# Gated mix of linear and softmax attention on one core: score groups of three and five, maxima units regrouped, one weight split on GpSimd, one PSUM pool fewer

## The chip, the cores and the metric

The kernel runs on one core of a Trainium2 chip. The engines of the core are PE (matmul, with its weight loads shown as PEld), DVE (vector), ACT (scalar), POOL (GpSimd) and SP, which here issues the DMA transfers. The metric is the device time of one execution in microseconds; the median of several runs counts.

## The reference

The input is x, 2048 tokens of 448 values. Two attentions with 16 heads of 28 run on it, and a gate mixes them, all in float32:

```
g   = sigmoid(x . gate_w)
A:  q, k, v = split(x @ A_wqkv);  pq, pk = q @ w_phi, k @ w_phi    (per head)
    phi = [softmax(p), softmax(-p)];  o = phi_q (phi_k^T v) / (phi_q sum(phi_k) + 1e-6);  a = o @ A_wo
B:  q, k, v = split(x @ B_wqkv);  o = softmax(q k^T * 28^-0.5) v;                       b = o @ B_wo
out = g * a + (1 - g) * b
```

Softmax is taken with its row maximum subtracted. In A that is cheap, as a row has 28 values; in B a row has 2048 scores, and the kernel finds the maxima in a pass of its own.

## The kernel before

Products of two float32 numbers are done in up to three matmul passes: every operand is split into a high part and the low rest (`XH`, `XL`; a weight has both parts side by side). `split_weight` (L141) writes the high part by a copy on ACT (L143) and the low part by a subtraction on DVE (L144); both engines can be given as arguments.

The order of the instructions on PE, DVE, ACT and POOL is that in which the program writes them (`manual_schedule`, L51); only the order of the transfers on SP is found by the planner. What stands ahead in a queue therefore holds what stands behind it.

**The front, 0 to some 336 us.**

- `proj_qk` (L577) makes queries and keys of B, 28 tiles of 11 passes each. ACT copies the high part of a tile (L589), DVE subtracts the low part (L590), and both go to DRAM (`qkd`).
- The loop over `i` (L727) has t = i and q = i − 16. For t below 16 it makes keys of A and their features (`features1`, `features2`, L438 to L462, on ACT, DVE and POOL), values of A (`value_a`), and adds to the key-value sums (`kv_add`). For q from 0 to 15 it makes queries and their features. From q = 3 it turns the features (`turn`, L515), multiplies them with the sums (`numer`), divides (`normalize1` to `normalize4`, whose last step writes `oTa` on POOL, L429), and multiplies with the output weight (`out_a`, tiles `poa`). From q = 18 it also makes the values of B (`value_b`, tiles `pvb`). Late in this loop, POOL's share is the feature subtraction (L447, L449), the feature product (L461) and `oTa`.
- At q = 2, the turn, the pools of the first half close and those of the second open. The PSUM pool is closed and opened there too, with four `s` banks in place of three and a `pv` bank.
- Forty-four **maxima units** (`mx_unit`, L259) lie between these pieces. A unit is four small matmuls into two double banks: `pmb` holds the scores against one half of a pair of key blocks, `pmd` those against the difference of the two. ACT takes the Relu of `pmd` (L288, `rl`), and two DVE instructions (L290) add `pmb` and keep the row maxima. The next unit's `pmb` waits for the Relu of the unit before it, its `pmd` for that unit's last reduce. Keys of a unit are prepared by two POOL subtractions (L221). `pace` and `tick` (L719) place one unit inside the matmul passes of a key and value pass; others stand at the head of steps, behind the feature work, or behind `out_a`.

**The main part, from some 336 us.** A step s (0 to 255) is one block of 128 keys against 512 queries for four heads. `scores` (L879) issues four matmuls into four PSUM banks (L885) and four exps on ACT (L903), whose results are kept in `p` tiles. `values` (L1010) of the step before adds eight small-column matmul pieces (L1017) into the `pv` bank. One `mx_visit` (L305) per step finds maxima for later heads: four matmuls `pm` (L322) into four banks, one `rl` on ACT from the first (L326), and DVE reduces (L333, L330, L336). The seven banks that scores and visits share stand in the list `free`; `mx_banks` takes four from its head, and `scores` puts used banks back in an order that sets which reader each later matmul waits for. Below s = 191 each step has four scores, values, visit. From 191, when `TWO` is reached, two steps' scores go together, with one visit, until the visits end; output projections (`project`, L1022) stand between the last steps.

Of the kernel before, what the change touches and what calls it, by code (L numbers as in the profile page):

```python
# [14 lines left out]
PSUM = bass.MemoryType.PSUM  # L15
DRAM = bass.MemoryType.DRAM

P = 128
S = 2048
D = 448  # L20
# [4 lines left out]
NT = S // P  # L25
# [15 lines left out]
def gated_mix_kernel(ctx, tc, xT, wqkB, wvB, wvA, wkAT, wqAT, phi, woA, woB,  # L41
# [17 lines left out]

    psn = [3, 2]  # L60

    def ps_s(nm):
        return ps.tile([P, 512], F32, tag="s", name=nm, bufs=psn[0])

    def ps_pv(nm):
# [546 lines left out]
    def split_part(w, key, n, i, low=nc.vector):  # L612
        split_weight(w, raws[key][i], slice(2 * i, 2 * i + 2), slice(0, n), low)

    def splits(n):

# [47 lines left out]
    for n in range(4, NP):  # L664
        take_acts()
        if n in (4, 5):
            x_loads(n - 2)
        if n == 8:
            nc.sync.dma_start(phi_s, phi)
            load_fold(wkAT, "k")  # L670
        if n == 10:
            part_loads("wB1", wqkB[:, :, 512:896], 384, "wB1")
        splits(n + 1)
        if n == 14:
            part_loads("wvA", wvA, 450, "wvA")
            nc.sync.dma_start(sel_s, sel)
            nc.sync.dma_start(mask_s, mask)
            for v in vap:
                nc.gpsimd.memset(v[:, :, 28:32], 0.0)
                nc.gpsimd.memset(v[:, :, 28:29], 1.0)  # L680
            feats = [bd.tile([P, H, 64], F32, name=f"feat{i}") for i in range(4)]
            for f in feats:
                nc.gpsimd.memset(f[:, :, 56:], 0.0)
        if 16 <= n < 20:
            mx_unit()
        proj_qk(n, ev)
        if n in (16, 18):
            split_part(wvA_s, "wvA", 450, (n - 16) // 2)
            take_lows()
        if 12 <= n < 16:  # L690
            fold(wkA_s, "k", n - 12)
        if n == 10:
            pair_query(0, 0)
            pair_load(0, 0)
        if n == 15:
            pair_load(0, 1)
            pair_query(0, 1)
        if n in (14, 19):
            take_subs()
# [27 lines left out]
    for i in range(2 * NT + 11):  # L727
        t, q = i, i - NT
        y = q - 1
        tb = y // 2  # L730
        take_acts()
        if t < NT and t % 2 == 0:
            mx_unit()
            passes = (55 if t < NT - 4 else 44) + (4 if t >= 4 else 0)
            pace["n"], pace["at"] = 4 if t >= 4 else 0, [passes // 2]
        if q in (0, 1):
            take_exps()

        if t % 2 == 0 and 0 <= t - 4 < NT:
            kv_add(t - 4)  # L740
            kv_add(t - 3)
        if q == 2:
            bk_s.close()
            ta_s = ExitStack()
            ta = ta_s.enter_context(tc.tile_pool(name="ta", bufs=1, reuse_waits="tile"))
            stg = ta_s.enter_context(tc.tile_pool(name="stg", bufs=2, reuse_waits="tile"))
            KV = ta.tile([P, 512], F32, name="KV")
            kvT = kv_copy()
            ps_s_.close()
            ps = ps_s_.enter_context(tc.tile_pool(name="psq", bufs=1, space=PSUM, reuse_waits="tile"))  # L750
            psn[0] = 4
            woA_s = weights(3, "woA_s")
            wvB_s = weights(2, "wvB_s")
            take_exps()
        if t < NT:
            pk = ps_s(f"pk{t}")
            tok_major(pk, t, wkA_s, D, tick)
            fk[t] = features1(pk, f"k{t}", nc.gpsimd)
            take_exps(1)
        if 0 <= q < NT:  # L760
            pq = ps_s(f"pq{q}")
            tok_major(pq, q, wqA_s, D)
        if q == 0:
            fk[NT - 1] = features2(fk[NT - 1], f"k{NT - 1}")
        if q in (1, 2):
            fq[q - 1] = features2(fq[q - 1], f"q{q - 1}")
        if 0 <= q < NT:
            fq[q] = features1(pq, f"q{q}", nc.vector if 0 < q < 9 else nc.gpsimd)
        if 0 <= t - 1 < NT - 1:
            fk[t - 1] = features2(fk[t - 1], f"k{t - 1}")  # L770
        if q in (0, 1) or q >= 8:
            mx_unit()
        if y >= 9 and y % 2 and tb - 4 < 8:
            oTs[tb - 4] = normalize4(ta, num.pop(tb - 4), f"a{tb - 4}", 2)
# [24 lines left out]
        if q == 2:  # L799
            raws["woA"] = [load_woA(b) for b in (0, 2)]  # L800
        if q == 11:
            part_loads("wvB", wvB, D, "wvB")
        if q in (4, 6):
            split_part(woA_s, "woA", D, (q - 4) // 2)
        if q in (14, 17):
            split_part(wvB_s, "wvB", D, (q - 14) // 3)
        if q == 1:
            gates()
        if y < 9 or y % 2:
            if y >= 2 and y - 2 < NT:  # L810
                turn(y - 2)
        if 0 <= y - 10 < NT:
            out_a(y - 10)
            out_a2(y - 10)
        if y >= 9 and y % 2 == 0 and y - 2 < NT:
            turn(y - 2)
        if NT + 3 <= q < NT + 10:
            mx_unit()
        if q == NT + 2:
            bd_s.close()  # L820
            vb = [value_tile(0)]
        if 0 <= q - NT - 2 < 8:
# [56 lines left out]
    def scores(s, i):  # L879
# [8 lines left out]
        if s == 0:  # L888
            p = at.tile([P, 2, 512], F32, tag="pp", name=f"p{s}_{i}", bufs=2)
            st = ps_mx(f"st{s}_{i}", i)  # L890
            for jl in range(2):
                score(2 * i + jl, st[:, jl, :])
            nc.scalar.activation(p, st, AF.Exp, scale=SCALE)
            pts.setdefault(s, []).extend([p[:, 0, :], p[:, 1, :]])
            return
        sts = []
        for j in (2 * i, 2 * i + 1):
            used.append(free.pop(0))
            sts.append(bank(used[-1], f"st{s}_{j}"))
            score(j, sts[-1])  # L900
        for j, st in enumerate(sts, 2 * i):
            p = p_slot(f"p{s}_{j}")
            nc.scalar.activation(p, st, AF.Exp, scale=SCALE)  # L903
            pts.setdefault(s, []).append(p)
        if i == 1:
            a, m = used[:], held[:]
            if s < TWO:
                free.extend([a[0], m[0], a[1], m[1], a[2], a[3], m[2]] if m else a)
            elif s % 2:
                free.extend([m[0], a[0], m[1], a[1]] if m else a)  # L910
                rest.extend([m[2], a[2], a[3]] if m else [])
            else:
                free.extend(rest + a)
                rest.clear()
            used.clear()
            held.clear()

    qst = [stack("qst0", False)]
    kst = [stack(f"kst{i}", True) for i in range(5)]
# [27 lines left out]

    free, used, held = list(range(7)), [], []  # L950
    spare, rest = [], []

    def bank(i, nm):
        return ps2.tile([P, 512], F32, tag=f"g{i}", name=nm, bufs=1)

    def mx_banks(f, first):
        b = [free.pop(0) for _ in range(4)]
        free.append(b[0])
        held.extend(b[1:])
        order = [first] + sorted({0, 1, 2, 3} - {first}, key=lambda j: j == first - 1)  # L960
        return [bank(b[order.index(j)], f"pm{f}_{j}") for j in range(4)]

# [59 lines left out]
    def project(qb, oT, tl):  # L1022
# [1 line left out]
        t = qb * 4 + tl  # L1024
        acc = acc_of[qb][:, tl, :]
        b = free.pop(0)
        free.append(held.pop(0) if held else b)
        if free[-1] != b:
            held.insert(0, b)
# [109 lines left out]
    for s in range(NS + 16):  # L1139
        take_acts()  # L1140
        if s < NS:
# [105 lines left out]
```

## Time and profile before

| | us |
|---|---|
| median of 3 runs | 1017.42 |
| lowest and highest run | 1017.32, 1019.32 |
| the profiled execution | 1015.89 |
| its span, first to last instruction | 1014.1 |
| granted PE clock | 1.000 |

Busy time in the span: PE 1002.8, ACT 815.7, DVE 679.7, PE's weight loads 561.9, POOL 236.0. A busy PE is not PE at its peak: the end of a matmul is modelled, so a small delay of the next one hides inside it. Delays of that size are therefore read from the starts of instructions, and larger ones from the waits. The timeline joins instructions of one kind that follow one another into one row, with their number at its end; the brackets tell how long the engine sat idle before it and what ended that.

### The profile page before, as it was taken

Reading aid. Unit: us, or ns where it says so; the run is one execution under the profiler, and the core shown is the slowest. Engines: PE = TensorE matmul, PEld = TensorE weight load, DVE = VectorE, ACT = ScalarE, POOL = GpSimd, SP = SyncE. Lnnn points to the kernel's source line nnn. Section 1 sums busy time; section 2 is a strip of 40 time slices with the busy share of each in tenths; the row PEclk is TensorE's granted clock in tenths of the full one; section 3 lists DMA queues with packets and bytes.
Section 4 is the critical chain, followed back from the end, with each engine's and each line's share of the span. In section 5 each row is a group of like instructions: output and inputs, shape, how many; then the busy total and the mean of one; then the engine's idle time right before and its main releaser. Section 6 shows DMA issues by size and latency. Waiting matters only on the chain.

```text
span 1014.1 us, 17989 instructions
## 1 busy us (share of the span) xinstructions
PE 1002.8 (99%) x6472; PEld 561.9 (55%) x6472; DVE 679.7 (67%) x1340; ACT 815.7 (80%) x1534; POOL 236.0 (23%) x213
## 2 busy tenths in 40 slices
PE   9999999999999999999999999999999999999998
PEld 8878888868779433343333334333333344454656
DVE  6466666997753578888887888788888874544202
ACT  5445445678762899999999999999999999979682
POOL 1235456588435102111011110101201011001010
PEclk9999999999999999999999999999999999999999
DMA  8973110132245703233622223522323345615131
GB/s 295 311 241 93 60 50 3 44 90 83 93 129 128 155 20 84 64 73 69 128 65 70 55 58 79 127 65 55 87 56 76 75 101 155 157 34 150 57 109 55
DMA packets 64250, 98.89 MB, mean 98 GB/s; under 512 B 18176, under 2 KB 24944, under 8 KB 64160
## 3 DMA queue, kind: packets, MB, share of 16 engines
q1 hardware_dynamic: 64160, 97.74, 35.9%
q8 instruction: 51, 0.84, 0.4%
q14 instruction: 39, 0.32, 0.1%
HBM read 69.54 MB, written 27.78 MB: 96 GB/s over the span
## 4 chain that ended last, share of the span: by engine, by line
PE 90%; DVE 5%; DMA 2%; ACT 1%; POOL 1%; issue 1%; SPq 0%; DVEq 0%; POOLq 0%; ACTq 0%
PE st L885 29%; PE pv L1017 25%; PE pm L322 9%; PE pk L127 4%; PE pva L127 4%; PE poa L109 4%; PE pqk L109 3%; PE pob L109 3%; PE pvb L109 2%; PE pvb L127 2%; PE pq L109 2%; DMA qkd<-ev 1%; PE pmb L285 1%; PE pqk L652 1%; DVE fsumq L459 1%; DVE rl L290 1%
## 5 line engine op out<-in xcount | busy, mean ns | idle before, releaser
L903 ACT ACTIVATE p<-st 128x512 f32<-128x512 f32 x1020 | 522.4, 619 | 25.9 <-PE st L885 25.8
L333 DVE TENSOR_REDUCE part<-pm 128x1 f32<-128x512 f32 x477 | 304.6, 685 | 150.3 <-PE pm L322 144.3
L885 PE MATMUL st<-qst,kst 128*128 128x512 f32 x1024 | 309.8, 429 | 0.9 <-ACT vb L715 0.5
L1017 PE MATMUL pv<-p,vb 128*32 128x512 f32 x2048 | 266.1, 603 | 0.0
L885 PEld LDWEIGHTS st<-qst,kst 128*128 128x128 f32 x1024 | 174.2, 187 | 120.0 <-issue 52.4
L322 PEld LDWEIGHTS pm<-kc,qc 28*128 28x128 f32 x848 | 40.5, 181 | 177.8 <-ACT p L903 150.9
L326 ACT ACTIVATE rl<-pm 128x512 f32<-128x512 f32 x212 | 126.9, 598 | 10.8 <-PE pm L322 0.7
L420 POOL TENSOR_TENSOR oUb<-oUb,rsb 128x512 f32<-128x512 f32 x15 | 19.3, 1289 | 462.3 <-DMA rsb<-rdb 328.9
L330 DVE CUSTOM_DVE_ANT_0 rl<-pm,rl 128x512 f32<-128x512 f32 x159 | 108.1, 680 | 0.0
L322 PE MATMUL pm<-kc,qc 28*128 28x512 f32 x848 | 106.8, 495 | 0.0
L1017 PEld LDWEIGHTS pv<-p,vb 128*32 128x32 f32 x2048 | 45.5, 108 | 73.6 <-issue 67.4
L290 DVE CUSTOM_DVE_ANT_0 rl<-pmb,rl 128x512 f32<-128x512 f32 x88 | 57.0, 685 | 29.4 <-ACT rl L288 29.4
L109 PE MATMUL pqk<-XH,wB 128*128 128x512 f32 x192 | 59.3, 397 | 0.0
L288 ACT ACTIVATE rl<-pmd 128x1024 f32<-128x1024 f32 x44 | 45.2, 1028 | 12.0 <-PE pmd L285 5.6
L589 ACT CAST ev<-pqk 128x512 fp32r<-128x512 f32 x28 | 16.1, 588 | 35.2 <-PE pqk L109 24.9
L109 PE MATMUL poa<-woA_s,oTa 128*128 128x448 f32 x192 | 43.5, 374 | 0.2 <-POOL oTa L429 0.2
L109 PEld LDWEIGHTS pqk<-XH,wB 128*128 128x128 f32 x192 | 35.4, 188 | 8.5 <-issue 1.5
L1032 DVE SCALAR_TENSOR_TENSOR acc<-pob,gate,acc 128x448 f32<-128x448 f32 x12 | 8.2, 684 | 47.2 <-PE pob L109 47.2
L196 POOL TENSOR_TENSOR kc<-kc,kd 28x512 fp32r<-28x512 f32 x12 | 15.3, 1277 | 102.2 <-DMA kc<-qkd 85.7
L109 PEld LDWEIGHTS poa<-woA_s,oTa 128*128 128x128 f32 x192 | 34.9, 188 | 6.6 <-issue 3.3
L109 PE MATMUL pq<-wqA_s,XH 128*128 128x448 f32 x128 | 37.3, 374 | 0.8 <-DVE ev L590 0.8
L127 PE MATMUL pk<-wkA_s,XH 128*128 128x448 f32 x128 | 37.9, 377 | 0.0
(161 smaller groups left out, 1153.3 us busy)
## 6 DMA issues: line engine op xcount, KB each, us to landing
qkd<-ev SPq DMA_DIRECT2D x28, 512.0 KB
qst<-qkd SPq DMA_DIRECT2D x64, 224.0 KB
kst<-qkd SPq DMA_DIRECT2D x64, 224.0 KB
od<-oTb SPq DMA_DIRECT2D x48, 112.0 KB
rsa<-rda SPq DMA_DIRECT2D x8, 512.0 KB
rsb<-rdb SPq DMA_DIRECT2D x15, 256.0 KB
kc<-qkd SPq DMA_DIRECT2D x64, 56.0 KB
gad<-ga SPq DMA_DIRECT2D x16, 224.0 KB
```

What stands on the lines that cost most here:

```text
L109: nc.tensor.matmul(dst, l, r, start=i == 0, stop=i == len(todo) - 1)
L127: nc.tensor.matmul(dst[:, :n], l, r, start=i == 0, stop=i == len(todo) - 1, skip_group_check=True)
L288: nc.scalar.activation(rl, pd, AF.Relu)
L290: nc.vector.tensor_tensor_reduce(rl[:, i, :], pb[:, i, :], rl[:, i, :], 1.0, LOWEST, ALU.add, ALU.max, part[:, col + i:col + i + 1])
L322: nc.tensor.matmul(pm[j], mxs[("qc", gq)][js, qt * P:(qt + 1) * P], mxs[("kc", g, kb)][js, :], start=True, stop=True, tile_position=(32 * ...
L326: nc.scalar.activation(rl, pm[kb], AF.Relu if kb < 3 else AF.Copy)
L330: nc.vector.tensor_tensor_reduce(r, pm[j], r, 1.0, LOWEST, ALU.add, ALU.max, part[:, col + j:col + j + 1])
L333: nc.vector.tensor_reduce(part[:, col + j:col + j + 1], pm[j], AX.X, ALU.max)
L420: (nc.gpsimd if n == 1 else nc.vector).tensor_mul(oU, oU, rs)
L885: nc.tensor.matmul(st, kst_of[(g, kt // 4)][:, j, (kt % 4) * P:(kt % 4 + 1) * P], qst_of[gq][:, j, :], start=True, stop=True)
L903: nc.scalar.activation(p, st, AF.Exp, scale=SCALE)
L1017: nc.tensor.matmul(pv[32 * j:32 * j + 32, :], vb[kt // 8][:, kt % 8, 4 * g + j, :], pt[j], start=kt == 0, stop=kt == NT - 1, tile_position ...
```

## The change

- **Groups of scores.** Up to s = 190, an odd step issues three scores and an even step five: the fourth of the odd step and the four of its own. Values and one visit follow behind each group. `score_group` takes the place of `scores` for all but s = 0, takes the list of (step, head) pairs and issues each exp directly behind its score. It also orders `free` for each size of group: visits now leave all four banks in `mb`, and a group merges them with its own.
- **PSUM at the turn.** The pool is kept. From the turn on, `turn4` makes every fourth request for an `s` bank take the `pv` bank.
- **A weight split.** Both parts of the split of `wvA` (at n = 16 and 18 of the projections) move to POOL, copy and subtraction.
- **Maxima units.** In the passes of t = 4, 6 and 8 two units are placed, at a third and at two thirds, where one was placed at half. The unit behind the features runs from q = 11 on and no more at q = 8, 9, 10. The second unit per step of q = 19 to 25 is gone. The last units therefore fall behind the opening of the pool `psv` and inside the value passes of t = 8 to 14.
- **Another split.** The split of `wvB` stands at q = 13 and 15 and not at 14 and 17.

```diff
+    turn4 = []
     def ps_s(nm):
+        if turn4:
+            turn4.append(nm)
+            if len(turn4) % 4 == 0:
+                return ps_pv(nm)
         return ps.tile([P, 512], F32, tag="s", name=nm, bufs=psn[0])
...
         if n in (16, 18):
-            split_part(wvA_s, "wvA", 450, (n - 16) // 2)
+            split_part(wvA_s, "wvA", 450, (n - 16) // 2, nc.gpsimd, nc.gpsimd.tensor_copy)
...
-            pace["n"], pace["at"] = 4 if t >= 4 else 0, [passes // 2]
+            pace["n"] = 4 if t >= 4 else 0
+            pace["at"] = [passes // 3, 2 * passes // 3] if t in (4, 6, 8) else [passes // 2]
...
-            ps_s_.close()
-            ps = ps_s_.enter_context(tc.tile_pool(name="psq", bufs=1, space=PSUM, reuse_waits="tile"))
-            psn[0] = 4
+            turn4.append("")
...
-        if q in (0, 1) or q >= 8:
+        if q in (0, 1) or q >= 11:
             mx_unit()
...
-        if q in (14, 17):
-            split_part(wvB_s, "wvB", D, (q - 14) // 3)
+        if q in (13, 15):
+            split_part(wvB_s, "wvB", D, (q - 13) // 2)
...
-        if NT + 3 <= q < NT + 10:
-            mx_unit()
...
+    def score_group(sc):
+        n, take = len(sc), []
+        def pop(k):
+            got = [free.pop(0) for _ in range(k)]
+            take.extend(got)
+            return got
+        if not mb or n == 4:
...
+        elif n == 3:
+            free.extend(last)
+            last.clear()
+            u = pop(3)
+            free.extend([mb[0], mb[1], u[0], mb[2], u[1], mb[3], u[2]])
+        elif n == 5:
+            free.extend(mb[:2])
+            u = pop(5)
+            free.extend([u[0], mb[2], u[1], mb[3], u[2]])
+            last.extend(u[3:])
+        else:
...
+        mb.clear()
+        for (s, j), i in zip(sc, take):
+            gq, kt = divmod(s, NT)
+            st = bank(i, f"st{s}_{j}")
+            nc.tensor.matmul(st, kst_of[(gq // NQ, kt // 4)][:, j, (kt % 4) * P:(kt % 4 + 1) * P],
+                             qst_of[gq][:, j, :], start=True, stop=True)
             p = p_slot(f"p{s}_{j}")
             nc.scalar.activation(p, st, AF.Exp, scale=SCALE)
             pts.setdefault(s, []).append(p)
...
+    turn4.clear()
...
-    free, used, held = list(range(7)), [], []
-    spare, rest = [], []
+    free, mb, last, spare = [0, 2, 3, 4, 5, 1, 6], [], [], []
...
         b = [free.pop(0) for _ in range(4)]
-        free.append(b[0])
-        held.extend(b[1:])
+        mb.extend(b)
...
-            for z in ([s] if s < TWO else [s, s + 1][:NS - s] if s % 2 else []):
-                if z:
-                    scores(z, 0)
-                    scores(z, 1)
+            if s and s < TWO:
+                score_group([(s, j) for j in range(3)] if s % 2
+                            else [(s - 1, 3)] + [(s, j) for j in range(4)])
+            elif s % 2:
+                score_group([(z, j) for z in (s, s + 1) if z < NS for j in range(4)])
```

More of the change, by code (lines that the diff above doesn't have):

```diff
@@ L610, in part_loads, with split_part @@
         loads(key, lambda: load_part(src, n, nm, 0), lambda: load_part(src, n, nm, 2))
-    def split_part(w, key, n, i, low=nc.vector):
-        split_weight(w, raws[key][i], slice(2 * i, 2 * i + 2), slice(0, n), low)
+    def split_part(w, key, n, i, low=nc.vector, high=nc.scalar.copy):
+        split_weight(w, raws[key][i], slice(2 * i, 2 * i + 2), slice(0, n), low, high)
     def splits(n):
@@ L894, in scores @@
             pts.setdefault(s, []).extend([p[:, 0, :], p[:, 1, :]])
[L895 to L901, printed above, removed]
+    def score_group(sc):
[7 more added lines that the diff above has]
+            last.clear()
+            pop(min(n, 4))
+            free.extend(take)
+            if n == 8:
+                u = pop(4)
+                free.extend(u)
+        elif n == 3:
+            free.extend(last)
+            last.clear()
+            u = pop(3)
[6 more added lines that the diff above has]
+        else:
+            free.extend(last + mb[:1])
+            last.clear()
+            u = pop(4)
+            free.extend([mb[1], u[0], mb[2], u[1]])
+            v = pop(4)
+            free.extend([mb[3], u[2], u[3]] + v)
+        mb.clear()
[4 more added lines that the diff above has]
+                             qst_of[gq][:, j, :], start=True, stop=True)
             p = p_slot(f"p{s}_{j}")
@@ L904, in scores @@
             pts.setdefault(s, []).append(p)
[L905 to L916, printed above, removed]
     qst = [stack("qst0", False)]
@@ L1026, in project @@
         b = free.pop(0)
-        free.append(held.pop(0) if held else b)
-        if free[-1] != b:
-            held.insert(0, b)
+        free.append(mb.pop(0) if mb else b)
+        if mb:
+            mb.insert(1, b)
         po = bank(b, f"pob{t}")
```

## The prediction

> **What bounds the kernel now.** I read the page first, then the stretches (busy time by window), the waits of PE, the timeline of one steady step, and the timelines around each PE stall of the front.
>
> ```profile
> span 1014.1 us, 17989 instructions
> PE 1002.8 (99%) x6472; PEld 561.9 (55%) x6472; DVE 679.7 (67%) x1340; ACT 815.7 (80%) x1534; POOL 236.0 (23%) x213
> ...
> 200.00:250.00 50.00, 47.70 (x380) 37.80 (x378) 43.35 (x85) 39.28 (x64) 42.57 (x32) 1.00 0.29 83
> ...
> 400.00:450.00 50.00, 50.00 (x309) 19.63 (x306) 40.17 (x81) 48.90 (x97) 8.80 (x10) 1.00 0.35 82
> ...
> PE pmd L285 <- DVE part L290: 4.3, 4, 2.1
> ...
> PE poa L109 <- POOL oTa L429: 0.2, 1, 0.2
> ...
> L903 ACT ACTIVATE p<-st 128x512 f32<-128x512 f32 x1020 | 522.4, 619 | 25.9 <-PE st L885 25.8
> ```
>
> In a window row the numbers after the length are busy us of PE, PEld, DVE, ACT, POOL, then the granted clock (1.00), DMA share and GB/s. PE is never idle from 400 to 450, so the steady loop has no wait that the busy time shows: a late matmul is hidden inside the modelled length of the one before it. ACT is at 48.90 of 50 there. In 200–250 PE loses 2.3 us and POOL is at 42.57 of 50. The waits rows (total, times, longest) are PE stalls of the front; the last row gives the mean exp, 619 ns.
>
> One step (timeline: start, length, engine, line):
>
> ```profile
> 507.17 1.24 PE L885 MATMUL st<-qst,kst 128*128 128x512 f32 x4
> 507.26 0.60 ACT L326 ACTIVATE rl<-pm 128x512 f32<-128x512 f32 x1
> 507.76 2.06 ACT L903 ACTIVATE p<-st 128x512 f32<-128x512 f32 x4
> 507.91 0.19 PEld L885 LDWEIGHTS st<-qst,kst 128*128 128x128 f32 x1 [0.22 <-ACT rl L326]
> 508.34 1.06 PE L1017 MATMUL pv<-p,vb 128*32 128x512 f32 x8
> 509.33 0.51 PE L322 MATMUL pm<-kc,qc 28*128 28x512 f32 x4
> 509.77 1.25 PE L885 MATMUL st<-qst,kst 128*128 128x512 f32 x4
> 509.87 0.60 ACT L326 ACTIVATE rl<-pm 128x512 f32<-128x512 f32 x1
> ...
> 520.20 1.25 PE L885 MATMUL st<-qst,kst 128*128 128x512 f32 x4
> ```
>
> From 507.17 to 520.20 are five steps: 2.606 us each, 5.21 a pair. In each, the weight load of the fourth score waits for the visit's `rl` (507.26 + 0.60 = 507.86; the load starts at 507.91), because that score gets the bank which `rl` reads. The loop closes: load 507.91, pv 508.34 (+0.43), pm 509.33 (+0.99), rl 509.87 (+0.54), its end +0.60 and the next load +0.05: 2.61, one step. ACT looks full (its last exp ends at 507.76 + 2.06 = 509.82, 0.05 before `rl`) and is not: the pitch of the exps is (2.06 − 0.62) / 3 = 0.48, so `rl` could start one pitch after the last exp's start, at 509.68, 0.2 sooner than it does.
>
> What does the late load cost?
>
> ```profile
> 507.73 0.68 PE L885 MATMUL st<-qst,kst 128*128 128x512 f32 x2
> 507.95 0.46 PE L885 MATMUL st<-qst,kst 128*128 128x512 f32 x1
> ...
> 955.08 0.39 PE L885 MATMUL st<-qst,kst 128*128 128x512 f32 x1
> 955.40 0.62 PE L1017 MATMUL pv<-p,vb 128*32 128x512 f32 x2
> ```
>
> At 955.08 the last score is not late and pv follows 0.32 behind it. At 507.95 it follows 0.39 behind (508.34). So the late load costs 0.07, between 0.06 and 0.08 by the rounding, though the score itself comes at its pitch (507.73 to 507.95, 0.22). That is what one late load costs the loop.
>
> **The change, part by part.**
>
> **Groups of three and five (steps 1 to 190, 95 pairs).** The instructions are the same in number; their order and banks change. After the three (odd step) come values and visit A; then five scores, the first of which is the fourth of the odd step, values, visit B. I follow the banks through the new list. The three take the banks of the last exps of the five before; the five take, in order, a bank freed by an exp, by a reduce of visit B, by an exp, by `rl` of A, by the first reduce of A. So the load that waits for `rl` comes once a pair instead of twice, and it is the fourth of five. PE from the first score to pv is now 508.34 − 507.17 = 1.17, of it 0.56 to the third score, 0.22 to the fourth, 0.39 to pv; twice, 2.34. After: three on time 0.56 + 0.32 = 0.88; five with one late load 1.17 + 0.22 or 0.23, 1.40; together 2.28. The saving is 0.06 to 0.07 a pair, one late load: 95 × 0.065 = 6.2 us. Bounds: nothing, if the wait costs the same wherever it falls, and 95 × 2 × 0.07 = 13 if neither load is late any more. I take one load of two, because `rl` of A ends as far behind its pm (0.54 + 0.60) as today, and the fourth of five stands where the fourth of four stood.
>
> What is queued behind: ACT runs three exps, `rl` A, five exps, `rl` B. `rl` A waits for nothing but its pm. The first exp of the five ends near pm + 0.54 + 0.60 + 0.48 = 1.62; the values that need it start at pm + 0.44 (509.33 to 509.77) + 1.40 = 1.84: 0.2 spare. `rl` B comes up to 0.26 later than today, with five exps ahead of it; its readers are the pm and reduces of the next visit, a step away. DVE is busy 2.1 of 2.6 (40.17 of 50), so the reduces that two of the five wait for keep 0.5 a step to spare: 0. The third of the three waits for the fifth exp and may be a few hundredths late: 0. If these covers go, each 0.1 costs what it costs in rival (b). From step 191 the banks fall as before: 0.
>
> **One weight split on POOL (n = 16, 18).**
>
> ```profile
> 53.14 0.95 ACT L143 CAST wvA_s<-wvA_raw 128x900 fp32r<-128x900 f32 x1 [0.60 <-DMA wvA_raw<-in_wvA_dram]
> 54.12 1.09 DVE L144 TENSOR_TENSOR wvA_s<-wvA_raw,wvA_s 128x900 fp32r<-128x900 f32 x1 [0.86 <-ACT wvA_s L143]
> 55.06 0.51 PE L285 MATMUL pmb<-kp,qp 28*128 28x512 f32 x2
> 56.49 0.50 PE L285 MATMUL pmd<-kp,qp 28*128 28x512 f32 x2 [0.92 <-DVE part L290]
> ...
> 58.76 0.69 DVE L290 CUSTOM_DVE_ANT_0 rl<-pmb,rl 128x512 f32<-128x512 f32 x1
> 59.13 2.64 POOL L221 TENSOR_TENSOR kp<-kp,kt 28x512 fp32r<-28x512 f32 x2 [11.27 <-DMA kt<-qkd]
> ...
> 64.09 0.50 PE L285 MATMUL pmd<-kp,qp 28*128 28x512 f32 x2 [0.71 <-DVE part L290]
> ...
> L428 POOL CAST oTb<-oUb x15: 609/610/615, 397.0 to 973.3; 128x512 fp32r<-128x512 f32 x15
> ...
> L461 POOL TENSOR_TENSOR feat<-feat,fsumk 128x896 f32<-128x896 f32 x16 | 27.3, 1704 | 2.5 <-DVE fsumk L460 0.8
> ```
>
> ACT's copy (0.95) and DVE's subtraction (1.09) stand ahead of the units' Relu and reduces, whose end the next pmd awaits. PE loses 56.49 − 55.06 = 1.43 there (pmb and pmd otherwise start together), of which the view shows 0.92 idle; at 64.09, by the same 0.5 hidden, 1.2. Both stalls, 2.6, go. On POOL the subtraction takes 1.7 (L461, as many elements) or more, the copy 1.07 (610 ns for 512 elements, scaled to 900): say 3.1 a split, two of them, from 53.14 to about 59.3. POOL idled 11.27 up to 59.13, so its key subtractions (L221, 2.64) slip by 0.2, to 61.9; but PE now reaches the unit that needs them (its pmb started 1.2 before 64.09) 1.4 sooner, at 61.5. So 0.5 of the stall stays: gain 2.1; bounds 0 (POOL 2 later still) and 2.6. The weight itself is read only by the value passes, behind the whole first key pass.
>
> [...]
>
> **PSUM set kept at the turn.**
>
> ```profile
> 184.39 0.67 PE L109 MATMUL pq<-wqA_s,XH 128*128 128x448 f32 x2 [0.81 <-DVE ev L590]
> ```
>
> The pq of q = 2 waits for the last projection's subtraction, since the new pool puts it on that bank. Without a new pool the fourth `s` bank is the old `pv` one, and this pq's bank was evacuated a unit earlier. Gain 0.8; bounds 0 (another evacuation is as late) and 0.8.
>
> **Maxima units regrouped.** Three units leave q = 8, 9, 10 for the passes of t = 4, 6, 8; the second units of q = 19 to 25 go; the last three follow the start of the last value passes.
>
> ```profile
> 211.19 0.50 PE L285 MATMUL pmb<-kp,qp 28*128 28x512 f32 x2
> 213.80 0.50 PE L285 MATMUL pmd<-kp,qp 28*128 28x512 f32 x2 [2.10 <-DVE part L290]
> ...
> 215.28 1.70 POOL L461 TENSOR_TENSOR feat<-feat,fsumq 128x896 f32<-128x896 f32 x1 [1.95 <-DVE dena L408]
> 223.56 2.51 POOL L429 TENSOR_TENSOR oTa<-oUa,oTa 128x512 fp32r<-128x512 f32 x2
> 224.88 1.29 PE L109 MATMUL poa<-woA_s,oTa 128*128 128x448 f32 x5 [0.20 <-POOL oTa L429]
> ...
> 277.99 0.49 PE L285 MATMUL pmb<-kp,qp 28*128 28x512 f32 x2
> 278.14 0.18 PEld L285 LDWEIGHTS pmd<-kp,qp 28*128 28x128 f32 x2
> ```
>
> The unit at 211.19 stalls PE 2.6, and the first poa loses some 0.4 at 224.88 to `oTa`. But `oTa` (223.56) stands at the end of POOL's chain of feature products, and that sets when poa can go: POOL idled 1.95 at 215.28 behind DVE, which the units' reduces had delayed. Without them I get `oTa` some 2.2 sooner. Of these, 1.4 is unit work that PE now does elsewhere (three units, under 0.5 each). So 0.8 of 3.0 is gained; bounds 0 and 3.0. The six passes with two units lose 0.15 each (277.99 to 278.14): 0.9. New: in t = 4, 6, 8 two units stand some 3.3 apart (fifteen passes and the unit), and a unit frees its banks 58.76 + 0.69 − 56.49 = 2.96 after its pmd. Its Relu also stands ahead of key and value evacuations on ACT, its reduces ahead of DVE's feature sums. I put 0.5 (bounds 0 and 3). The last units stand beside the value passes, clear of the first scores, which wait for the reduces of the unit before the last and for the last Relu, each over a microsecond earlier by the order of passes. The units' key and query loads move with them on SP's queue; the rows they fetch are read a group later: 0. Net 0.8 + 0.9 − 0.5 = 1.2; bounds −2.1 and 3.9.
>
> **`wvB` split at q = 13 and 15.**
>
> ```profile
> 255.96 2.59 DVE L144 TENSOR_TENSOR wvB_s<-wvB_raw,wvB_s 128x896 fp32r<-128x896 f32 x1
> 258.75 0.50 PE L285 MATMUL pmb<-kp,qp 28*128 28x512 f32 x2
> 259.83 0.50 PE L285 MATMUL pmd<-kp,qp 28*128 28x512 f32 x2 [0.58 <-DVE part L290]
> ```
>
> The 2.59 delays the unit's reduces: pmd is 1.08 late. A step earlier it stands in a step with one unit and no `oUa` product. DVE still has it in one piece. Gain 0.9; bounds −1 (it delays another unit as much) and 1.1.
>
> **Sum.** Front 2.1 + 0.8 + 1.2 + 0.9 = 5.0 (bounds −3.1 and 8.4). With the main loop 11.2. The profiled execution took 1015.89 (span 1014.1 and 1.8 around it), 1.5 below the median of the runs; 1004.7 on its scale, 1017.42 − 11.2 = 1006.2 on the median's.
>
> **The rivals.**
>
> (a) *The late load costs nothing that comes back.* Its wait only moves: the loop load, pv, pm, `rl` closes over a pair just as over a step. Then the front alone counts: 1017.42 − 5.0 = 1012.4. For it: the load at 507.91 lies wholly beside the matmul that began at 507.73. Against: 0.39 against 0.32. [...]
>
> (b) *Slower: the exp of the fourth score holds the values.* It now comes right ahead of the values that use it, with 0.2 spare, and none of it shows today, where four exps have a step's time. Each 0.1 past the spare costs 9.5 us over 95 pairs. It decides from 0.12 past it (0.065 of the loop and 0.053 of the front eaten). At 0.18, the net is 95 × 0.115 = 10.9 lost and 5.0 gained: 1023.
>
> (c) *POOL becomes the front's bound.* Splits at 2.4 and copies slower than I scaled put the key subtractions past the next units, and POOL at 42.57 of 50 takes back the regrouping: the front gives 0, main 6.2: 1011.2; at the front's lower bound of −3.1, 1014.3.
>
> (d) *Neither load is late:* 13 from the loop, 1017.42 − 13 − 5 = 999.4.
>
> **How the numbers follow.** Mine 0.52 (its own range 1003 to 1010: 0.05 to 0.08 a pair, front 3 to 7), (a) 0.14, (b) 0.16, (c) 0.10, (d) 0.08. Changes within 0.2% (2 us) can't be told from none. Of (a) 0.03 and of (c) 0.03 fall there, of (c) 0.02 are slower, and of (b) 0.01 within and 0.15 slower: faster 0.76, same 0.07, slower 0.17. The range 1000.5 to 1015.5 holds mine, (a), (c) and the start of (d).
>
> **What would show it.** Scores in groups of 3 and 5, two steps summing to about 5.15; weight loads of scores that wait for `rl` once per pair; ACT idle ahead of `rl` A, none ahead of B. Of PE's waits for L290 in the front, those at 55, 63, 211 and 259 gone, pq's gone; poa waiting for POOL more than 0.2. I am wrong if pv or its loads wait for exps (b), if a pair still takes 5.22 (a), or if units in t = 4, 6, 8 or the key subtractions show new waits over 2 us in sum (c).

## The result and the profile after

The changed kernel takes 1009.54 us (median of 6 runs, 1008.56 to 1010.06), the kernel before 1017.37 (median of 6, 1016.89 to 1019.32): ratio 0.992, with an interval of 0.9908 to 0.9933. It is 7.8 us faster where 11.2 were forecast. The profiled execution took 1009.49; its span is 1007.7.

The page of the changed kernel, its first lines and two groups:

```profile
span 1007.7 us, 17959 instructions
PE 998.3 (99%) x6472; PEld 556.3 (55%) x6472; DVE 677.6 (67%) x1338; ACT 803.5 (80%) x1532; POOL 241.8 (24%) x217
...
L332 ACT ACTIVATE rl<-pm 128x512 f32<-128x512 f32 x212 | 132.2, 624 | 15.7 <-PE pm L328 13.9
```

ACT now idles 15.7 us in all ahead of `rl`, nearly all of it for its own pm; in the pair below it is 0.18 ahead of A, and none ahead of B. One pair of steps in the timeline (line numbers are six higher than before in the front and in the visits, and differ more behind them: L937 is a score, L940 its exp, L1041 the values, L328 the visit, L332 its `rl`):

```profile
500.93 1.49 PE L937 MATMUL st<-qst,kst 128*128 128x512 f32 x5
501.03 0.60 ACT L332 ACTIVATE rl<-pm 128x512 f32<-128x512 f32 x1 [0.18 <-PE pm L328]
501.52 2.55 ACT L940 ACTIVATE p<-st 128x512 f32<-128x512 f32 x5
501.68 0.32 PEld L937 LDWEIGHTS st<-qst,kst 128*128 128x128 f32 x2 [0.22 <-ACT rl L332]
502.35 1.06 PE L1041 MATMUL pv<-p,vb 128*32 128x512 f32 x8
503.34 0.51 PE L328 MATMUL pm<-kc,qc 28*128 28x512 f32 x4
503.78 0.97 PE L937 MATMUL st<-qst,kst 128*128 128x512 f32 x3
503.91 0.66 ACT L332 ACTIVATE rl<-pm 128x512 f32<-128x512 f32 x1
504.68 1.06 PE L1041 MATMUL pv<-p,vb 128*32 128x512 f32 x8
506.11 1.48 PE L937 MATMUL st<-qst,kst 128*128 128x512 f32 x5
```

From 500.93 to 506.11 a pair takes 5.18 (over many pairs 5.17) where it took 5.21 to 5.22. One load a pair waits for `rl`: the fourth of the five, at 501.68.

The front, PE's waits between 40 and 340 us:

```profile
PE pft L531 <- POOL feat L467: 2.3, 1, 2.3
PE pmd L291 <- ACT fT L534: 0.8, 1, 0.8
PE poa L115 <- POOL oTa L435: 0.6, 1, 0.6
PE pn L545 <- ACT fT L534: 0.3, 1, 0.3
```

Here `pft` are the features being turned and `pn` their products with the sums. The four waits of 4.3 for L290 and the wait of the turn's pq are gone; a new one of 2.3 stands near 215, where the old one of 2.1 stood near 212.

To see where the front's time went, the table gives the lengths of its stretches. Each is the difference between the starts of two matmuls in the trace: one matmul in the middle of the projections' thirteenth tile (at 36.30 in the profile of before), the first key pass of A (64.52), the eleventh (135.86), the third query pass (184.39), the tenth (208.79), the second `poa` (231.55), the sixth, the eighth, the last, the first score, and the values of step 1. Two executions with the front of before are beside the profile of before: one from the first experiment, one from the kernel before with half an `rl`.

| us, from ... to | before, profiled | before's front, 1st exp. | before's front, half `rl` | after |
|---|---|---|---|---|
| projections to first key pass (wvA) | 28.22 | 27.13 | 27.16 | 25.77 |
| key passes 1 to 11 (units at t = 4, 6, 8) | 71.34 | 71.28 | 71.37 | 73.27 |
| to third query pass (turn) | 48.53 | 48.53 | 48.53 | 47.65 |
| to tenth query pass | 24.40 | 24.33 | 24.39 | 24.19 |
| to second poa (POOL's chain) | 22.75 | 23.57 | 23.55 | 23.25 |
| to sixth poa | 24.58 | 24.58 | 24.58 | 24.58 |
| to eighth poa (wvB) | 9.97 | 9.97 | 9.98 | 10.59 |
| to last poa (second units gone) | 46.72 | 47.27 | 47.58 | 43.83 |
| to first score (last units) | 19.18 | 19.18 | 19.18 | 20.86 |
| to values of step 1 | 6.75 | 6.75 | 6.69 | 5.99 |
| sum | 302.44 | 302.59 | 303.02 | 300.00 |

Against the first experiment's column the front is 2.6 shorter. Ahead of the table the profiles differ too: its first mark lies at 36.30 in the profile of before and at 36.2 to 37.4 in the others.

The last column is one execution, and a short one. Two others have the same front: the second experiment, and the changed kernel with half an `rl`. Their sums are 300.99 and 302.47. They took 25.79 and 26.82 to the first key pass, and 44.50 and 45.19 from the eighth to the last `poa`. A term that is read from one of these two stretches is therefore good to about 1 us only, and the front as a whole is better taken from its own run.

### The profile page after: what moved, and what is told of

Same layout as the page of the kernel before. It is cut to its first block, busy times and chain, and to the rows that moved or that the text cites. A ratio compares the mean times of both kernels' runs of the same rounds, so it can differ in the third digit from the quotient of the medians.

```text
span 1007.7 us, 17959 instructions
## 1 busy us (share of the span) xinstructions
PE 998.3 (99%) x6472; PEld 556.3 (55%) x6472; DVE 677.6 (67%) x1338; ACT 803.5 (80%) x1532; POOL 241.8 (24%) x217
## 4 chain that ended last, share of the span: by engine, by line
PE 95%; DVE 3%; POOL 1%; issue 0%; ACT 0%; DMA 0%; DVEq 0%; POOLq 0%; ACTq 0%
PE st L937 28%; PE pv L1041 25%; PE pm L328 9%; PE pqk L115 6%; PE poa L115 4%; PE pk L133 4%; PE pva L133 4%; PE pob L115 3%; PE pvb L133 2%; PE pq L115 2%; PE pvb L115 2%; PE pmb L291 2%; PE pqk L658 1%; PE pkv L485 1%; PE pft L531 1%; PE poL L1079 1%
## 5 line engine op out<-in xcount | busy, mean ns | idle before, releaser
L940 ACT ACTIVATE p<-st 128x512 f32<-128x512 f32 x1020 | 529.3, 639 | 25.8 <-PE st L937 25.8
L937 PE MATMUL st<-qst,kst 128*128 128x512 f32 x1020 | 303.4, 424 | 0.3 <-DVE acc L1056 0.3
L1041 PE MATMUL pv<-p,vb 128*32 128x512 f32 x2048 | 266.1, 603 | 0.0
L937 PEld LDWEIGHTS st<-qst,kst 128*128 128x128 f32 x1020 | 168.0, 187 | 99.3 <-ACT p L940 48.6
L332 ACT ACTIVATE rl<-pm 128x512 f32<-128x512 f32 x212 | 132.2, 624 | 15.7 <-PE pm L328 13.9
L328 PEld LDWEIGHTS pm<-kc,qc 28*128 28x128 f32 x848 | 40.5, 181 | 177.8 <-issue 104.8
L336 DVE CUSTOM_DVE_ANT_0 rl<-pm,rl 128x512 f32<-128x512 f32 x159 | 108.3, 681 | 0.0
L328 PE MATMUL pm<-kc,qc 28*128 28x512 f32 x848 | 107.2, 495 | 0.0
L1041 PEld LDWEIGHTS pv<-p,vb 128*32 128x32 f32 x2048 | 45.4, 108 | 94.3 <-issue 87.6
L115 PE MATMUL pqk<-XH,wB 128*128 128x512 f32 x192 | 59.3, 397 | 0.0
L596 DVE TENSOR_TENSOR ev<-pqk,ev 128x512 fp32r<-128x512 f32 x28 | 19.0, 690 | 29.1 <-ACT ev L595 29.0
```

The costliest lines, as they stand in the source:

```text
L115: nc.tensor.matmul(dst, l, r, start=i == 0, stop=i == len(todo) - 1)
L328: nc.tensor.matmul(pm[j], mxs[("qc", gq)][js, qt * P:(qt + 1) * P], mxs[("kc", g, kb)][js, :], start=True, stop=True, tile_position=(32 * ...
L332: nc.scalar.activation(rl, pm[kb], AF.Relu if kb < 3 else AF.Copy)
L336: nc.vector.tensor_tensor_reduce(r, pm[j], r, 1.0, LOWEST, ALU.add, ALU.max, part[:, col + j:col + j + 1])
L937: nc.tensor.matmul(st, kst_of[(gq // NQ, kt // 4)][:, j, (kt % 4) * P:(kt % 4 + 1) * P], qst_of[gq][:, j, :], start=True, stop=True)
L1041: nc.tensor.matmul(pv[32 * j:32 * j + 32, :], vb[kt // 8][:, kt % 8, 4 * g + j, :], pt[j], start=kt == 0, stop=kt == NT - 1, tile_position ...
```

## The experiments

Each run is timed beside the kernel before on the same chip; the four groups of runs had 1017.89, 1016.75, 1017.47 and 1017.90 for it.

**The groups of scores alone.** Everything of the diff that concerns the front is taken back; `score_group`, `mx_banks`, `project` and the loop over steps stay.

> Only the score groups of three and five; the whole front as before. Theory: one late weight load less per pair, as the trace of the changed kernel shows it: a pair of steps at 5.17 us against 5.22, 95 times 0.05, so 4.5 to 5 us faster than before. Rival 1: the forecast's 0.065 a pair, 6.2. Rival 2: the steady loop is worth nothing of its own and all of the measured 7.8 comes from the front: within 1 us of before.

Measured 1012.58, ratio 0.995 (0.9937 to 0.9963), 5.1 us faster by the ratio. A pair takes 5.17. The theory holds; rival 1 lies within the interval as far as the time goes, but not by the pair.

**The front alone.** All front edits on the kernel before, scores in fours.

> All four changes of the front, scores in fours as before. Theory: the front gains what is left of 7.8 after the groups, 2.5 to 3.5 us, with PE idle some 2.3 us near 215 behind POOL's feature product and the granted clock down to a half behind that. Rival: the front alone gains the forecast's 5.0 and something of it is given back at the start of the main part: 5 faster here, steps of 2.61 as before.

Measured 1014.25, ratio 0.9966 (0.9954 to 0.9979), 3.5 faster; steps of 2.61, PE idle 2.32 near 215. The rival's 5 lies outside the interval (2.1 to 4.7). The two parts add: 5.1 and 3.5, with 8.1 for both by the ratio.

**The regrouped units alone.** The edits of `pace`, of `q >= 11` and of `NT + 3 <= q` on the kernel before.

> Only the regrouped maxima units, everything else as before. Theory: the idle of 2.3 us near 215 comes with the regrouping, since DVE's low part of the output weight now falls behind a POOL product that began just ahead of it: it shows here too, and the kernel is between 1 us faster and 1 us slower than before. Rival: the idle is an accident of the shifted times and needs the other edits too: it does not show here, and the kernel is 1.5 to 2.5 us faster.

Measured 1018.27, ratio 1.0006 (0.9995 to 1.0018): no gain. An idle of 3.3 is there, but not the one expected. DVE's subtraction began ahead of the POOL product here (211.27 against 211.50) and took its usual 1.03, and the wait is another. Timeline of this kernel:

```profile
220.32 1.78 DVE L420 TENSOR_TENSOR oUa<-oUa,rsa 128x1024 f32<-128x1024 f32 x1 [1.81 <-DMA rsa<-rda]
222.14 1.14 ACT L428 CAST oTa<-oUa 128x512 fp32r<-128x512 f32 x2 [4.34 <-DVE oUa L420]
224.65 1.60 PE L539 MATMUL pn<-fT,KV 56*32 56x256 f32 x32 [3.27 <-ACT fT L528]
```

DVE stood still 1.81 for the transfer of the first division's factors (`rsa`), ACT 4.34 for DVE's product, and the copies of turned features that stand behind it on ACT held PE. So a stall comes with the regrouping even alone, and its form depends on the timing.

**The split of wvA alone.** `split_part(wvA_s, ..., nc.gpsimd, nc.gpsimd.tensor_copy)` on the kernel before.

> Only the split of wvA on POOL. Theory: both PE stalls at 55 and 63 go and the first key pass starts 2.4 us sooner; nothing behind it takes this back: 2 to 2.6 us faster. Rival: POOL's key subtractions come late by what was gained, or the time is lost again at the turn: within 1 us of before.

Measured 1016.73, ratio 0.9988 (0.9977 to 0.9999), 1.2 faster: between theory and rival. The stretch to the first key pass takes 25.79, as in the changed kernel. In its profiled run 1.3 was lost again in the stretch with POOL's chain, beside a PE clock of 0.50 (last section), and more near 280, where DVE waited 1.93 for `rsa`.

**Output weight of A split sooner.**

```diff
-        if q in (4, 6):
-            split_part(woA_s, "woA", D, (q - 4) // 2)
+        if q in (3, 4):
+            split_part(woA_s, "woA", D, q - 3)
```

> The changed kernel with the two splits of the output weight of A one and two steps sooner (q = 3 and 4 in place of 4 and 6), so that no low part falls into the step at 209 us. Theory: PE's idle of 2.3 us near 215 comes from that subtraction of DVE, which began just behind a POOL product and ended 0.95 after it; without it DVE's chain is 2.6 us shorter, the idle falls under 0.8, and the slow clock behind it goes too: 2.5 to 4 us faster than the changed kernel, 1006 to 1007. Rival: POOL's chain and the division's transfers bound the first output products anyway: the idle moves to them, the kernel stays within 1 us of 1009.5.

Measured 1011.91, ratio 0.995 (0.9931 to 0.9968), by the medians 2.4 slower than the changed kernel. The idle near 215 is gone, 0.4 is left near 208; but PE idles 3.28 at 222 and 2.08 at 268. The idle moves, as the rival has it, but the kernel does not stay within 1 us. Its runs go with their mean granted clock: 1007.88 and 1010.17 at 0.998, 1014.23 and 1014.84 at 0.995.

**Its second half later.** `q in (4, 7)` in place of `(4, 6)`.

> The changed kernel with the second split of the output weight one step later (q = 7 in place of 6). Theory: the subtraction then stands behind the next feature sums, where DVE has less work before the first division: the idle near 215 falls to under 1 us, 1 to 3 us faster than the changed kernel. Rival: the same pair of POOL product and subtraction meets one step later and the idle only moves: within 1 us of 1009.5.

Measured 1011.13, ratio 0.9943 (0.9931 to 0.9955), 1.6 slower than the changed kernel by the medians, which neither the theory nor the rival has. Again the idle only moves, from pft (0.47 left) to pn:

```profile
217.33 1.19 DVE L426 TENSOR_TENSOR oUa<-oUa,rsa 128x1024 f32<-128x1024 f32 x1
218.56 1.14 ACT L434 CAST oTa<-oUa 128x512 fp32r<-128x512 f32 x2 [3.78 <-DVE oUa L426]
221.07 1.96 PE L545 MATMUL pn<-fT,KV 56*32 56x256 f32 x32 [2.64 <-ACT fT L534]
```

**Half an `rl`, in both kernels.** Lines L326, L330 and L336 (and their like in the changed kernel) work on `[:, :256]`.

> The kernel before with the visits' rl, and what reads it, on half of the columns (512 to 256): the maxima of these blocks come from half of their keys, that part is left out. rl then ends some 0.25 us sooner and the fourth score's weight load is not late. Theory: a late load costs 0.065 a step, the step falls from 2.606 to 2.54 us, 190 times: 12 us faster. Rival: the loop closes over something else (exps, DVE), the step stays at 2.59 or more: under 3 us faster.

Measured 1008.43, ratio 0.9917 (0.9904 to 0.993), 8.4 faster (interval 7.1 to 9.8): more than the rival, less than the theory's 12. The step is 2.56.

> The changed kernel with the same half rl (that part of the maxima left out). Theory: only one load a pair is late here, so the pair falls by half of what the kernel before gains, from 5.17 to 5.10 or 5.12 us: 5 to 6 us faster than the changed kernel, and the pair is as long as two steps of the kernel before with half rl. Rival: the groups of three and five have a cost of their own: the pair stays longer than those two steps by over 0.03.

Measured 1004.65, ratio 0.9875 (0.9861 to 0.9889), 4.9 less than the changed kernel, just under the theory's 5 to 6. Timeline of the kernel before with half `rl`, one of its steps, then a pair of the changed kernel with it:

```profile
502.73 1.20 PE L885 MATMUL st<-qst,kst 128*128 128x512 f32 x4
503.86 1.06 PE L1017 MATMUL pv<-p,vb 128*32 128x512 f32 x8
```

```profile
501.42 1.45 PE L937 MATMUL st<-qst,kst 128*128 128x512 f32 x5
502.80 1.06 PE L1041 MATMUL pv<-p,vb 128*32 128x512 f32 x8
504.23 0.96 PE L937 MATMUL st<-qst,kst 128*128 128x512 f32 x3
505.12 1.07 PE L1041 MATMUL pv<-p,vb 128*32 128x512 f32 x8
```

From the first score to pv: four scores 1.13, five 1.38, three 0.89. Over the 170 to 180 groups of the loop between 345 and 800 us the means are:

| first score to pv, us | full `rl` | half `rl` | one late load |
|---|---|---|---|
| four scores (before) | 1.179 | 1.131 | 0.048 |
| five scores (after) | 1.411 | 1.362 | 0.049 |
| three scores (after) | 0.893 | 0.895 | none |

The loads agree. From 400 to 800 us the trace has 153 loads of scores that wait for `rl` in the kernel before, one a step, and 77 in the changed kernel, one a pair. With half an `rl` there are none in either. With no late load in either, a pair is 5.12 in the changed kernel and 2 × 2.561 = 5.12 in the one before. So the groups cost nothing of their own, and one late load costs 0.048 to 0.049. (In the kernel with the front alone four scores take 1.175, which would make it 0.044.) 190 × 0.048 = 9.1 lies within the interval of the kernel before with half an `rl`.

**wvB split as before.** `q in (14, 17)` in place of `(13, 15)`.

> The changed kernel with wvB split at q = 14 and 17 as before. Theory: the two splits at 13 and 15 each begin behind a POOL product and end late, which costs the changed kernel 0.6 us in place of the 0.9 gained: 0.5 to 1.5 us faster than the changed kernel, the wait of a pmd near 265 gone. Rival: the splits at 14 and 17 meet the same products, the stall of 1.1 near 259 comes back: 0 to 1 us slower.

Measured 1009.30, ratio 0.992 (0.9908 to 0.9933): the same as the changed kernel, and less than the theory's gain of 0.5 or more. The stretch with the splits takes 10.27 (10.59 there); the wait of 0.9 near 259 is back. In this profile the next stretch took 45.25 against 43.83, but so it did, with 45.19, in another execution of the changed front; the runs do not decide between the two places.

**ACT's order.**

```diff
+        turned = y >= 9 and y % 2 and y - 2 < NT
+        if turned:
+            take_exps(int(q < NT))
+            turn(y - 2)
         if y >= 9 and y % 2 and tb - 4 < 8:
             oTs[tb - 4] = normalize4(ta, num.pop(tb - 4), f"a{tb - 4}", 2)
...
-            if y >= 2 and y - 2 < NT:
+            if y >= 2 and y - 2 < NT and not turned:
                 turn(y - 2)
```

> The changed kernel with another order of ACT in every second step from q = 10: the exp of the features and the copies of the turned features go ahead of the high parts of oTa, which wait for DVE's division; PE, DVE and POOL keep the order of their engines but for the POOL subtraction behind that copy. Theory: the first idle (2.3 us, POOL's feature product behind DVE's late subtraction) stays, since ACT is not what it waits for; within 1 us of the changed kernel. Rival: ACT's wait of 2.9 us for the division holds the whole chain of features: 2 us or more faster.

Measured 1010.47, ratio 0.9926 (0.9913 to 0.994): as the theory has it, the 2.3 at pft stays, and PE now idles 2.1 at poa.

**Both.** That order, and `q in (4, 7)`.

> Both: that order of ACT, and the second split of the output weight at q = 7. Theory: with the subtraction away the only thing left that holds PE is ACT's wait for the division (3.8 us in the kernel with q = 7 alone, PE idle 2.6 behind it); with both gone PE's idle between 205 and 226 falls from 3 us to under 1.5 and the slow clock behind it goes: 2 to 4 us faster than the changed kernel, 1005.5 to 1007.5. Rival: POOL's own chain bounds the first output products: the idle moves to them, within 1 us of 1009.5.

Measured 1010.26, ratio 0.9927 (0.9915 to 0.994): the rival. PE's waits from 205 to 226 us:

```profile
PE poa L115 <- POOL oTa L435: 2.5, 1, 2.5
PE pn L545 <- ACT fT L534: 0.5, 1, 0.5
PE pft L531 <- POOL feat L467: 0.5, 1, 0.5
```

The first `poa` waits for `oTa`, which POOL begins at 221.70 (221.84 with the late split alone, 223.15 in the changed kernel). Between 212 and 221.70 POOL stands still 1 us here, and DVE not at all until 223.4. The four variants that remove one wait or two left PE 3.1 to 4.4 us of waits between 205 and 226, against 2.9 in the changed kernel. As far as these runs show, DVE and POOL bound the stretch together, and none of the four beats the changed kernel by the median.

**wvA back on ACT and DVE**, the rest as changed.

> The changed kernel with the split of wvA on ACT and DVE as before. Theory: this step is worth 1.4 us and not the 2.4 that the profile of the kernel before shows, because in that profile the weight's transfer landed late against PE; the stretch from the fourteenth projection tile to the first key pass takes 27.1 us here against 25.8 in the changed kernel, and the kernel is 1 to 1.8 us slower than the changed one. Rival: the profile of before is typical, the stretch takes 28.2 and the kernel is 2.4 slower.

Measured 1011.11, ratio 0.9933 (0.992 to 0.9945): 1.6 slower than the changed kernel by the medians, as the theory has it. The stretch (from the mark of the table, which lies in the thirteenth tile) takes 63.85 − 36.24 = 27.61 in its profile, 1.8 longer than in the changed kernel; between the first experiment and the changed kernel the same stretch differs by 1.4.

## Why the prediction was right, and where it was off

**The groups: mechanism right, size 0.049 and not 0.065.** 95 × 0.049 = 4.7, against 6.2. The two rows that gave the price were ends of a spread: pv follows a late last score by 0.379 on average (0.39 was read), a punctual one in the steady loop, with half an `rl`, by 0.327 (0.32 was read, far outside it). What was worked out around it held: one load of two, the fourth of five; the last exp that values wait for ends 502.12 ahead of 502.35, 0.23 spare against the 0.2 worked out; ACT idle ahead of `rl` A and not of B. Rivals (a), (b) and (d) fell: a pair is shorter by one late load, no value waits for an exp, and the second wait is left. The view does put the idle of 0.24 ahead of each group's first load down to an exp now; but the same 0.24 stood there before without one, and the first score starts 0.44 behind pm as before.

**wvA on POOL: right, 2.1 forecast, 1.2 to 1.8 found** (1.2 by its own run, 1.6 when taken back, 1.4 and 1.8 by the stretches). Timeline of the changed kernel:

```profile
52.78 0.94 POOL L149 CAST wvA_s<-wvA_raw 128x900 fp32r<-128x900 f32 x1 [5.39 <-DMA wvA_raw<-in_wvA_dram]
53.80 1.96 POOL L150 TENSOR_TENSOR wvA_s<-wvA_raw,wvA_s 128x900 fp32r<-128x900 f32 x1
56.72 1.95 POOL L150 TENSOR_TENSOR wvA_s<-wvA_raw,wvA_s 128x900 fp32r<-128x900 f32 x1
58.75 2.64 POOL L227 TENSOR_TENSOR kp<-kp,kt 28x512 fp32r<-28x512 f32 x2
62.33 0.49 PE L291 MATMUL pmd<-kp,qp 28*128 28x512 f32 x2
```

POOL took 2.9 a split (3.1 estimated), its key subtractions began at 58.75 (59.3), and the pmd that needs them came 0.2 late (0.5). The term was too large because the stall that it removes was: 28.22 in the profile of before, 27.13 and 27.16 in two other executions of the same front. The split waits for a transfer, and how late this stands against PE differs from run to run. This holds on POOL as well: in the changed kernel with half an `rl` POOL's first copy began at 54.16 and not at 52.78, and the stretch took 26.82.

**The turn: right.** 0.88 by the table, 0.8 forecast.

**The units: 1.2 forecast, 1.0 by the table, from other parts, and nothing by their own run.** The six double passes gave more: from the eighth to the last `poa` 3.4, of which three units are about 2.0, so 1.4 against 0.9; by the two other executions of this front it is 0.8 and 0.1. The three units in key passes cost 0.66 each, 2.0 together, where the forecast had 1.4 for their work and 0.5 for new waits. PE shows no wait there, so it is the price of a unit that was too low; why it is dearer there is not shown. The step that failed is that `oTa` comes 2.2 sooner. Counted from the start of the tenth query pass, POOL began it 223.56 − 208.79 = 14.77 later in the kernel before, and 223.15 − 207.88 = 15.27 later in the changed one: 0.5 later, though two units had left the stretch. By the table the stretch to the second `poa` fell by 0.3. The wait at 212 gave way to the one at 217 that the profile after shows. The reading that fits is that PE's stall in the kernel before had been hiding the time of DVE's and POOL's chain. Rival (c), that POOL takes back the regrouping, came true in this stretch, with DVE beside it. Unforeseen was a gain of 0.76 at the first exps, where the last units now stand ahead. Without it the table would leave the units 0.2; that their total came near the forecast is luck.

**wvB: 0.9 forecast, no gain found.** The stretch took 0.6 longer in the profile after, and still 0.3 longer with the splits back in their old places, where the kernel is as fast; so at most about 0.3 belongs to the places. In the changed kernel the subtraction is shorter (1.73 and 1.54) and meets the next transfer, in the timeline of the changed kernel:

```profile
260.03 1.54 DVE L150 TENSOR_TENSOR wvB_s<-wvB_raw,wvB_s 128x896 fp32r<-128x896 f32 x1
263.24 0.18 DVE L414 TENSOR_SCALAR dena<-dena 128x32 f32<-128x32 f32 x1 [1.66 <-DMA dena<-oUa]
265.02 0.50 PE L291 MATMUL pmd<-kp,qp 28*128 28x512 f32 x2 [0.78 <-ACT fT L534]
```

The timeline has DVE waiting 1.66 for the denominators, with a unit's reduces queued behind, and PE's pmd is late again. (The view names ACT for its 0.78; the last reduce of the unit before ends on DVE at 264.97, 0.05 ahead of this pmd.) The forecast asked what the subtraction delays, not what stands between it and the unit on DVE's queue.

**The sum.** Loop 4.7 to 5.1 against 6.2, front 2.6 by the table and 3.5 by its own run against 5.0. The bounds of the front (−3.1 and 8.4) held. The direction and the mechanism of the loop were right, and a late load was priced a third too high. In the front one gain did not come (`oTa`), one was a wait that is shorter in most executions (wvA), one came to nothing (wvB), and an unforeseen one made up for a part.

## What to carry to other kernels

Price a small delay that returns every step from the mean over many steps, and check it once by taking its cause away on half the data: that gave 0.048 and 0.049 in two kernels. A stall of one engine can hide that two others have no slack there; work moved out of such a stretch came back here as idle in another place (3.1 to 4.4 us of PE's waits in the four variants, 2.9 in the changed kernel), so count what the other engines do in it before booking the stall as a gain. A stall whose start was a transfer's arrival had the size of one execution only (a stretch of 28.22 in one, 27.13 and 27.16 in two others).

## What the runs showed of the hardware

**A DVE subtraction and a POOL product that overlap: whichever started second took longer, 2.62 us in place of 1.03 or 2.35 in place of 1.70.** The same subtraction with the same POOL product beside it, in the timeline of the kernel before, then in that of the changed one:

```profile
209.46 1.03 DVE L144 TENSOR_TENSOR woA_s<-woA_raw,woA_s 128x896 fp32r<-128x896 f32 x1
209.69 2.35 POOL L461 TENSOR_TENSOR feat<-feat,fsumq 128x896 f32<-128x896 f32 x1 [0.73 <-DVE fsumq L460]
```

```profile
208.98 1.70 POOL L467 TENSOR_TENSOR feat<-feat,fsumq 128x896 f32<-128x896 f32 x1 [0.73 <-DVE fsumq L466]
209.01 2.62 DVE L150 TENSOR_TENSOR woA_s<-woA_raw,woA_s 128x896 fp32r<-128x896 f32 x1 [0.18 <-issue]
...
214.96 0.12 DVE L414 TENSOR_SCALAR dena<-dena 128x32 f32<-128x32 f32 x1
...
249.84 1.68 DVE L414 TENSOR_SCALAR dena<-dena 128x32 f32<-128x32 f32 x1
```

In these rows the second ends behind the first by nearly what it takes when it starts first, as if it had waited for the first to end. In the changed kernel POOL's product ends at 210.68, and DVE's subtraction 0.95 later (1.03 in the kernel before, where it starts first); in the kernel before, DVE ends at 210.49 and POOL 1.55 later (1.70 in the changed kernel). DVE's instruction on `dena`, 0.12 at 214.96, lasts 1.68 at 249.84, where a POOL product runs (248.93 to 251.47), and ends at 251.52, 0.05 behind it. In the kernel before DVE starts first by 0.23 us, in the changed one POOL by 0.03; there DVE's subtraction is 1.6 us longer and POOL's product 0.65 shorter. Two of DVE's reduces show nothing of this: beside the POOL product at 215.19 in the changed kernel, which keeps its 1.70, they (L449 and L450, from 215.38) last 0.56 and 0.60, where their medians are 0.61 and 0.61. Why the second takes longer is not shown.

**The granted PE clock fell to 0.50 behind some idles of 2.1 to 2.3 us.** In the changed kernel PE's idle of 2.31 ended at 216.94. Windows of the changed kernel (the last but two is the granted clock):

```profile
214.00:216.00 2.00, 0.63 (x4) 0.23 (x2) 1.93 (x6) 2.00 (x4) 0.81 (x1) 1.00 0.77 207
216.00:218.00 2.00, 1.05 (x9) 1.06 (x9) 1.97 (x4) 0.10 (x1) 2.00 (x3) 0.92 0.24 61
218.00:220.00 2.00, 2.00 (x8) 1.79 (x7) 1.97 (x3) 1.04 (x2) 2.00 (x2) 0.50 0.10 9
220.00:222.00 2.00, 2.00 (x11) 1.52 (x9) 1.02 (x1) 1.97 (x5) 2.00 (x2) 0.73 0.18 51
```

For 3.4 us (what the shares 0.92, 0.50 and 0.73 add up to; windows of 0.2 us show 0.50 from 217.8 to 221.0 and 1.00 before 217.6 and from 221.2) PE runs at half its clock, and the query pass there takes 3.6 from its first matmul's start to its last one's (217.92 to 221.49) where one takes 2.2 (183.68 to 185.85). In the windows of the kernel with the split of wvA alone, the same follows an idle of 2.10, and lasts twice as long, 6.8 us:

```profile
212.00:216.00 4.00, 3.80 (x40) 2.14 (x41) 3.85 (x11) 2.10 (x4) 2.32 (x2) 0.50 0.50 129
216.00:220.00 4.00, 4.00 (x19) 3.40 (x17) 2.92 (x5) 1.86 (x5) 2.68 (x3) 0.68 0.21 34
```

Not every such idle was followed by a fall. The 2.10 in the profile of before was not (1.00 in every window from 208 to 226), nor was the 2.32 in the changed kernel with half an `rl` (mean clock 1.000). For the kernel before a mean clock of 1.000 is rare: of its 23 runs on one chip, three had it and took 1016.8 on average, sixteen had 0.998 and took 1017.8, four had 0.996 or 0.997 and took 1019.2.

A fall of 3.4 us did not cost the same with both fronts. With the front of before, the stretch from the tenth query pass to the second `poa` took 22.75 with no fall, 23.57 and 23.55 with one of 3.4 us, and 24.90 (the split of wvA alone) with one of 6.8; there `oTa` too begins 1.1 later than in the others, so not all of this need be the clock's. With the changed front it took 23.25 with a fall of 3.4 and 23.26 with none: without it PE waited longer, 1.2 in place of 0.6 for `oTa` and 0.8 for `fT`. There the slow clock cost nothing, which again speaks for DVE and POOL as the bound. Why the clock fell behind one such idle and not behind another, and for 3.4 us or twice that, no run here shows.
